# Loading the first pair of value heads as f32 over the two hardware DMA queues and casting it on GpSimd

## Chip, cores and metric

One NeuronCore of a Trainium2 chip. The metric is the device time of one execution in microseconds (us); lower is better.

## The reference, cut to what matters

```python
def _attn_ref(q, k, v, E, F):            # q, k, v: (8, 8, 1024, 64) f32; E, F: (64, 1024) f32
    k_proj = np.einsum('ks,bhsd->bhkd', E, k)
    v_proj = np.einsum('ks,bhsd->bhkd', F, v)
    scores = scale * np.matmul(q, k_proj.transpose(0, 1, 3, 2))
    ...                                   # softmax
    return np.matmul(attn, v_proj)

def _moe_ref(x, w_in, w_out):            # x: the 8192 x 512 result of the attention
    h = x @ w_in                          # w_in 512 x 2048
    g = h * np.clip(h + 3.0, 0.0, 6.0) / 6.0
    return g @ w_out                      # w_out 2048 x 512
```

A cheap attention with projected keys and values feeds two large matrix products. The products (lines 450 and 470 of the kernel before) fill TensorE from about 20 us to the end. The change touches only the loads of the first batch, by which the kernel gets to that point.

## The kernel before: the parts that matter

```python
    ef_f32 = consts.tile([P, S], f32, name="ef_f32")
    nc.sync.dma_start(out=ef_f32[:KP], in_=E)          # hardware queue of SyncE
    nc.scalar.dma_start(out=ef_f32[KP:], in_=F)        # hardware queue of ScalarE
    ...
    def load_pair(n, j):                               # GpSimd's queue: the DMA casts f32 to bf16
        hs = slice(2 * j, 2 * j + 2)
        nc.gpsimd.dma_start(out=kqv[0][n][:, hs], in_=kqv_dram[n][0][:, hs])

    for j in range(KO):                                # KO = 4 pairs of heads
        load_pair("k", j)
        load_q0(0, slice(2 * j, 2 * j + 2))
        ...
    for j in range(KO):
        load_pair("v", j)
    ...
    for lo, n in ((0, 128), (128, 128), (256, 256), (512, 256), (768, 256),
                  (1024, 512), (1536, 512)):
        load_w_in(lo, n)                               # also GpSimd's queue
    ...
            for j in range(KO):                        # First.first_block, cut
                self.keys(j)                           # needs k of pair j
                if j > 1:
                    sums(j - 2)
                self.queries(0, (j,))                  # needs q of pair j
                if j > 0:
                    scores(j - 1)
                ...
            self.vals(0, nc.vector.tensor_copy)        # needs v of pair 0
            ...                                        # vals(1), vals(2), products between them
            self.vals(3, nc.scalar.copy)
    # then the first matmul of x @ w_in (line 450), which needs the first piece of w_in
```

All loads that cast go by GpSimd's queue in this kernel; so all of q, k, v and the weights stand in one line, in the order of this code. "v0" below is v of the first pair of heads, "k3" is k of the last pair, and so on. The *start* is the time at which line 450 begins (457 in the changed kernel, whose lines are 7 lower). Some matmul records are missing from a trace: of the first two matmuls of this line, the profile before has only the second (20.68 us; the weights for both are loaded at 20.45). To compare like with like, "start" is the second one.

The softmax here doesn't subtract the row's maximum and nothing guards it: scores larger than these inputs give would overflow.

## Time and profile before

| | kernel before |
|---|---|
| time, median of the first 3 runs | 511.65 us (511.52 to 511.9) |
| span of the profiled run | 510.0 us, in a run of 511.81 us |
| TensorE busy | 497.4 us, 98% |
| start (first recorded matmul of line 450, its second) | 20.68 us |
| first piece of w_in landed | 20.41 us |

In the views PE is TensorE and PEld its weight loads, DVE is VectorE, ACT ScalarE, POOL GpSimd and SP SyncE; L450 is line 450 of the kernel. The lines of the page, of the chain, of the waits and of the first microseconds are in the prediction below. The point to take from them: after 20 us TensorE hardly ever waits, so the time of this kernel is, to a fraction of a microsecond, the start plus a constant. In the profiled run 511.81 - 20.68 = 491.13 us.

### The profile page before, as it was taken

Reading aid. Unit: us, or ns where it says so; the run is one execution under the profiler, and the core shown is the slowest. Engines: PE = TensorE matmul, PEld = TensorE weight load, DVE = VectorE, ACT = ScalarE, POOL = GpSimd, SP = SyncE. Lnnn points to the kernel's source line nnn. Section 1 sums busy time; section 2 is a strip of 40 time slices with the busy share of each in tenths; the row PEclk is TensorE's granted clock in tenths of the full one; section 3 lists DMA queues with packets and bytes.
Section 4 is the critical chain, followed back from the end, with each engine's and each line's share of the span. In section 5 each row is a group of like instructions: output and inputs, shape, how many; then the busy total and the mean of one; then the engine's idle time right before and its main releaser. Section 6 shows DMA issues by size and latency. Waiting matters only on the chain.

```text
span 510.0 us, 7106 instructions
## 1 busy us (share of the span) xinstructions
PE 497.4 (98%) x2750; PEld 224.3 (44%) x2802; DVE 257.5 (50%) x401; ACT 274.5 (54%) x493; POOL 37.9 (7%) x57
## 2 busy tenths in 40 slices
PE   8899999999899999999999999999999999999996
PEld 3444444444344444444444444444444444444442
DVE  3572735855655733656434743467444563334420
ACT  3657476567576545664466644674447654444431
POOL 8610020010100200002000020000000000000000
PEclk9999999999999999999999999999999999999999
DMA  9999999599299493516924188421110111101112
GB/s 165 199 205 207 202 156 236 97 159 176 88 184 186 91 218 76 125 41 91 225 57 94 52 141 169 107 58 33 42 41 25 38 42 42 42 21 42 41 51 74
DMA packets 74210, 55.39 MB, mean 109 GB/s; under 512 B 35520, under 2 KB 65984, under 8 KB 74176
## 3 DMA queue, kind: packets, MB, share of 16 engines
q0 software_dynamic: 31952, 29.36, 37.0%
q1 hardware_dynamic: 42000, 25.17, 19.4%
q10 hardware_dynamic: 224, 0.39, 0.3%
q8 instruction: 22, 0.36, 0.3%
q14 instruction: 12, 0.10, 0.1%
HBM read 59.24 MB, written 16.78 MB: 149 GB/s over the span
## 4 chain that ended last, share of the span: by engine, by line
PE 94%; DMA 3%; issue 1%; POOL 1%; DVE 0%; ACT 0%; DVEq 0%; POOLq 0%
PE mm L470 43%; PE mm L450 43%; PE at L181 3%; DMA w_in_sb<-in_moe_w_in_dram 2%; PE at L227 1%; PE mm L227 1%; DMA k<-in_k_dram 1%; PE at L209 1%; PE mm L209 0%; PE at L370 0%; POOL q L97 0%; DVE kp L187 0%; POOL k L101 0%; PE at L350 0%; DVE xT L246 0%
## 5 line engine op out<-in xcount | busy, mean ns | idle before, releaser
L456 DVE SCALAR_TENSOR_TENSOR g<-r,mm 128x512 bf16<-128x512 f32 x256 | 173.8, 686 | 131.8 <-ACT r L455 130.4
L470 PE MATMUL mm<-w_out_sb,g 128*128 128x512 bf16 x995 | 231.8, 379 | 1.7 <-issue 0.5
L450 PE MATMUL mm<-xT,w_in_sb 128*128 128x512 bf16 x1001 | 229.2, 379 | 3.1 <-DVE xT L246 1.2
L455 ACT ACTIVATE r<-mm 128x512 f32<-128x512 f32 x256 | 152.8, 599 | 76.2 <-PE mm L450 73.7
L450 PEld LDWEIGHTS <-w_in_sb 128*128 128x128 bf16 x1024 | 99.4, 98 | 124.0 <-issue 5.5
L470 PEld LDWEIGHTS <-g 128*128 128x128 bf16 x1024 | 98.0, 98 | 121.5 <-issue 7.2
L484 ACT COPY o_sb<-mm 128x512 f32<-128x512 f32 x35 | 20.3, 587 | 91.5 <-PE mm L470 91.5
L484 DVE COPY o_sb<-mm 128x512 f32<-128x512 f32 x28 | 19.3, 691 | 67.3 <-PE mm L470 64.2
L159 ACT ACTIVATE rec<-mm 128x512 f32<-128x512 f32 x34 | 19.0, 595 | 34.1 <-PE mm L227 17.6
L163 ACT ACTIVATE rec<-rec 128x512 f32<-128x512 f32 x60 | 35.6, 637 | 0.0
L246 DVE TENSOR_TENSOR xT<-at,rec 128x512 bf16<-128x512 f32 x44 | 28.1, 680 | 7.1 <-ACT rec L163 7.1
L218 ACT ACTIVATE aT<-at 128x512 bf16<-128x512 f32 x44 | 23.1, 613 | 0.9 <-PE at L209 0.9
L159 ACT ACTIVATE rec<-at 128x512 f32<-128x512 f32 x30 | 17.3, 598 | 6.0 <-PE at L227 3.7
L199 POOL COPY mark<-kT 1x1 bf16<-1x1 bf16 x5 | 0.9, 178 | 210.1 <-DMA kT<-kp 210.1
L181 PE MATMUL at<-k,e_t 128*64 128x512 bf16 x56 | 13.4, 382 | 0.0
L181 PE MATMUL at<-v,f_t 128*64 128x512 bf16 x56 | 13.4, 382 | 0.0
L187 DVE CAST kp<-at 64x512 bf16<-64x512 f32 x14 | 9.0, 678 | 4.9 <-PE at L181 4.9
L218 ACT ACTIVATE aT<-mm 128x512 bf16<-128x512 f32 x12 | 6.5, 594 | 8.9 <-PE mm L209 8.9
L190 DVE CAST vp<-at 64x512 bf16<-64x512 f32 x14 | 9.7, 694 | 0.4
L181 PEld LDWEIGHTS <-e_t 128*64 128x64 bf16 x56 | 5.6, 109 | 7.2 <-PE at L227 2.1
L479 DVE COPY o_sb<-mm 128x256 f32<-128x256 f32 x1 | 0.4, 425 | 16.0 <-PE mm L470 16.0
L227 PE MATMUL at<-aT,vp 64*64 64x512 bf16 x88 | 8.5, 376 | 0.0
(62 smaller groups left out, 147.0 us busy)
## 6 DMA issues: line engine op xcount, KB each, us to landing
out_dram<-o_sb SPq DMA_DIRECT2D x63, 256.0 KB, 2.0
k<-in_k_dram POOLq DMA_DIRECT2D x7, 1024.0 KB, 15.4
v<-in_v_dram POOLq DMA_DIRECT2D x7, 1024.0 KB, 21.0
q<-in_q_dram POOLq DMA_DIRECT2D x7, 1024.0 KB, 10.5
w_out_sb<-in_moe_w_out_dram POOLq DMA_DIRECT2D x4, 512.0 KB, 17.1
k<-in_k_dram POOLq DMA_DIRECT2D x4, 256.0 KB, 5.8
v<-in_v_dram POOLq DMA_DIRECT2D x4, 256.0 KB, 7.9
w_in_sb<-in_moe_w_in_dram POOLq DMA_DIRECT2D x2, 512.0 KB, 11.9
```

What stands on the lines that cost most here:

```text
L159: nc.scalar.activation(ln, den, AF.Ln)
L163: nc.scalar.activation(ln, ln, AF.Exp, scale=-1.0)
L181: nc.tensor.matmul(ps[e * KP:(e + 1) * KP], ef_t[e][:, so, :], kqv[self.b]["kv"[e]][:, :, so, :], start=(so == 0), stop=(so == SO - 1))
L190: nc.vector.tensor_copy(self.vp[a * KP:(a + 1) * KP], self.ps[KP:].rearrange("p (h d) -> p h d", d=D))
L218: nc.scalar.activation(self.aT[j][:, r].rearrange("p a n -> p (a n)"), tiles[r], AF.Exp, scale=scale)
L227: nc.tensor.matmul(tiles[t][c:c + D].rearrange("p (r n) -> p r n", r=2), stationary(r, 2 * j + a), self.aT[j][r:r + KP, :, a, :], start=Tr ...
L246: nc.vector.tensor_mul(self.xT[:, j, t, :], av[t], recs[t])
L450: nc.tensor.matmul(h_ps, w_in_sb[:, ko, fo * P:(fo + 1) * P], xT[:, ko, t, :], start=(ko == 0), stop=(ko == KO - 1))
L455: nc.scalar.activation(r, h_ps, AF.Relu, bias=0.5, scale=1.0 / 6.0)
L456: nc.vector.scalar_tensor_tensor(g[:, fo, :], r, 1.0, h_ps, op0=ALU.min, op1=ALU.mult)
L470: nc.tensor.matmul(o_ps, g[:, fo, c * P:(c + 1) * P], w_out_sb[:, fo, :], start=(fo == 0), stop=(fo == FO - 1))
L484: (copy or nc.scalar.copy)(o_sb, o_ps)
```

## The change

The intent: the hardware queues are idle after E and F, and the two GpSimd casts are cheap, so one pair of v can leave the crowded line of GpSimd's queue and everything behind it, w_in above all, can come earlier.

```diff
@@ -72,6 +72,11 @@
     nc.sync.dma_start(out=ef_f32[:KP], in_=E)
     nc.scalar.dma_start(out=ef_f32[KP:], in_=F)
+
+    v_f32 = []
+    for a, queue in enumerate((nc.sync, nc.scalar)):
+        v_f32.append(rpool.tile([P, TOK], f32, tag="r", name="r").rearrange("p (s d) -> p s d", s=SO))
+        queue.dma_start(out=v_f32[a], in_=kqv_dram["v"][0][:, a])
@@ -105,8 +110,10 @@
-    for j in range(KO):
+    for j in range(1, KO):
         load_pair("v", j)
+    for a in range(2):
+        nc.gpsimd.tensor_copy(kqv[0]["v"][:, a], v_f32[a])
```

## The prediction

> **What bounds the kernel now.** I read the page from the top: engine shares, slices, chain.
>
> ```profile
> PE 497.4 (98%) x2750; PEld 224.3 (44%) x2802; DVE 257.5 (50%) x401; ACT 274.5 (54%) x493; POOL 37.9 (7%) x57
> ...
> PE   8899999999899999999999999999999999999996
> ...
> DMA  9999999599299493516924188421110111101112
> ...
> PE 94%; DMA 3%; issue 1%; POOL 1%; DVE 0%; ACT 0%; DVEq 0%; POOLq 0%
> ```
>
> TensorE is busy for 98% of 510 us and holds 94% of the chain that ends last. Its only thin slices are the first two (12.75 us each) and the last. So a change to the very first loads can only move the moment at which TensorE begins its unbroken run, and everything after shifts by as much. The next view is therefore the chain of the first 24 us; columns are start, length, what.
>
> ```profile
> 4.73 6.02 DMA k<-in_k_dram
> 10.75 0.29 issue
> 11.04 9.37 DMA w_in_sb<-in_moe_w_in_dram
> 20.41 0.27 issue
> 20.68 0.38 PE mm L450
> ```
>
> The unbroken run starts at 20.68 us, released by the landing of the first piece of w_in at 20.41. That piece is issued at 11.04, when the third pair of k has landed (the program lets eight transfers of GpSimd's queue be open), but takes 9.37 us to land. It is not large (128 KB written as bf16): it stands in line behind what was issued before. The waits of TensorE between 14 and 24 us say how much that is worth.
>
> ```profile
> PE mm L450 <- DMA w_in_sb<-in_moe_w_in_dram: 0.7, 1, 0.7
> PE mm L370 <- ACT aT L390: 0.6, 1, 0.6
> PE mm L363 <- DVE kT L333: 0.3, 1, 0.3
> ```
>
> TensorE itself was ready 0.73 us before that landing: its timeline has the last matmuls of the values (line 338) at 19.33 for 0.62, so until 19.95. The front of the kernel thus has two chains that end almost together: the queue of loads (20.41) and the attention of the first block on TensorE, ScalarE and VectorE (19.95 plus a start).
>
> The stretches of the first microseconds (columns: window, its length, busy time and count of five engines, clock, DMA share, GB/s) show whether the transfer engines have room.
>
> ```profile
> 2.00:2.50 0.50, 0.50 (x3) 0.16 (x2) 0.00 (x0) 0.50 (x1) 0.50 (x2) 1.00 1.86 123
> 2.50:3.00 0.50, 0.50 (x2) 0.15 (x1) 0.00 (x0) 0.14 (x1) 0.49 (x2) 1.00 0.22 57
> 3.00:3.50 0.50, 0.50 (x2) 0.15 (x1) 0.00 (x0) 0.00 (x0) 0.43 (x2) 1.00 0.75 279
> 4.00:4.50 0.50, 0.50 (x3) 0.22 (x2) 0.00 (x0) 0.00 (x0) 0.50 (x2) 1.00 0.87 191
> 7.00:8.00 1.00, 0.93 (x10) 0.43 (x8) 0.42 (x1) 0.01 (x1) 1.00 (x2) 1.00 1.24 201
> ```
>
> From 4.5 us on the share is above 1 (packets overlap) and the rate is flat near 200 GB/s of bf16 written, which is 400 GB/s of f32 read. The engines are full; before 4.5 us there are holes.
>
> **What the Trainium skill says.** "DMA: Bandwidth & Descriptors", section "Issuing engines are not separate DMA queues": transfers begun by sync, scalar and gpsimd run on the same 16 engines and interleave, and several issuers only save issue time. Section "Queues, rings and completion order" of the same page: each engine takes packets in turn from the rows that have work. The trace agrees as far as it goes: the sum of the rates is flat while E, F and k are in flight together. "GPSIMD Engine Reference", section "4.1 Engine selection": one-input elementwise work is roughly line-rate on GpSimd, and section 3.1 gives 1.03 to 1.8 cycles an element at 1.2 GHz; the trace before has no such cast on GpSimd, only a memset of 128x128 in 0.23 us.
>
> **The change part by part.**
>
> 1. Removed: one of the four v loads of GpSimd's queue (0.74 us of issue at 7.58) and its place in the line. The landings (start plus time to landing, from the DMA issues of single windows) are k0 6.8, q0 7.6, k1 8.8, q1 9.5, k2 10.75, q2 11.5, k3 12.7, q3 13.4, v0 14.7, v1 16.0, v3 18.6, w_in 20.4 us. So one v pair takes 1.28 us of the line: 512 KB read in 1.28 us is 410 GB/s, the full rate.
>
> 2. Added: two loads of 256 KB f32 on the hardware queues, behind E and F. Issue costs 0.58 us on SyncE and on ScalarE, both idle then (both wait for E and F until 6.11). E's packets of 4 KB take 159 ns once the stream runs (my reading of the raw packet records), which is 412 GB/s over 16 engines: the same time for each byte read as the casting loads. So the same 1.28 us of engine time is still needed, only earlier: it is not taken away from the front of the kernel, because it is drawn from the same full engines before w_in. Only what falls into the holes is free. The holes from 2.5 to 4.5 us are 0.5 x (0.78 + 0.25 + 0 + 0.13) = 0.58 us; E needed 0.8 us from the end of its issue to its first packet, so the new load, issued until 1.9 us, cannot fill the first of them: I choose 0.25 us filled, with 0 to 0.5 possible. First piece of w_in: 20.41 - 0.25 = about 20.15 us.
>
> 3. Moved: k and q of all pairs come after (or between) the packets of v0, so they are late by 1.28 - 0.25, about 1.0 us: k0 7.8, q0 8.6, k1 9.8, q1 10.5, k2 11.75, k3 13.7, q3 14.4. Against the starts on TensorE: keys of pair 0 at 8.01 (k0 in time), of pair 1 at 9.70 (0.1 to 0.3 late), of pair 2 at 11.39 (0.4 to 0.6), of pair 3 at 13.01 (0.7 to 0.9). But after the keys of pair 3 TensorE waited 0.61 us for ScalarE until 14.26, and that wait absorbs the delay: keys 13.8 to 14.4, the sums at once after it, queries at 14.8 instead of 14.59. Left over: 0.2 to 0.45 us, call it 0.3. The chain on TensorE then ends at 19.95 + 0.3 = 20.25. The v pairs 1 to 3 keep their times less the filled hole (14.7 is passed by v0, which is already there), so they do not add.
>
> 4. Two casts of 128x512 f32 to bf16 on GpSimd. With the skill's 1.03 to 1.8 cycles, an estimate: 512 x 1.03 to 1.8 / 1.2 GHz = 0.44 to 0.77 us, plus a start, say 0.75 each. The compiled order puts them after the v issues and before w_in. The last v issue now waits for k1 (9.8) and ends at 10.5; casts until 12.0; then w_in is issued at 12.0, not 11.04. Cost on the path: none, since the line in front of it lasts until about 18.5; there are some 6 us of room. The values' first use is at 15.94, 4 us later. One slot fewer in the eight open transfers also means that w_in now waits for q1, not k2; that is earlier than the casts and does not count.
>
> 5. The r buffers: both loads sit in two of four buffers of r, free since 12 us, first wanted at 22.66. No cost.
>
> Sum: TensorE starts its run at the later of w_in (20.15 + 0.27) and its own chain (20.25 + some 0.2), so near 20.45 instead of 20.68: 0.2 us earlier, 0.04% of 511.65. Later loads keep their order and total. The first w_out chunk lands at 20.69 + 14.5 = 35.2 and is wanted at 35.66, so that small gain is not lost there. Predicted: 511.5 us.
>
> **The rivals.**
>
> A. The gain is real: v0 leaves the line, holes and slack hide its bytes, and w_in lands 1.28 us earlier. For it: the 0.73 us wait is measured. Against: the share above 1 from 4.5 us on. Even then TensorE was ready only at 19.95, so at most 0.7 us: 510.9.
>
> B. A wait takes the place: v0's packets push F and the first k and q back by the full 1.3 us (two hardware rows against one software row, no hole used). F landed at 6.05, 1.1 us after E, and starts the whole chain (casts at 6.11). If F is late by 0.5 to 1 us and k3 by 1.3, TensorE's chain ends at 20.8 to 21.2 and w_in no longer matters: plus 0.3 to 0.7, 511.9 to 512.4.
>
> C. GpSimd becomes the bound: a cast of over 3 us would delay w_in beyond its place in the line and the whole weight stream with it. Nothing in the trace speaks for it, a memset of a quarter of the columns took 0.23 us; if so, plus 1 to 3 us.
>
> D. Nothing moves at all: filled holes go to nobody because the slower chain is TensorE's. 511.6 to 511.7.
>
> **Range and chances.** The three mechanisms span 510.9 to 512.4; three runs before spread over 0.4 us, and another chip may differ by that again. I take 510.7 to 512.6. A 2% effect would be 10.2 us, half of the whole front of the kernel; only a hang-like wait on GpSimd's queue could do it. Faster 0.005, same 0.985, slower 0.01.
>
> **What would show it.** Right: the landing of the first w_in within 0.5 us of 20.4 in spite of v0's absence from its queue; k3 and q3 landing about 1 us later than 12.7 and 13.4; casts under 1 us, ended by about 12.5; the first matmul of line 450 (then a few lines lower) between 20.2 and 20.9; TensorE's wait for w_in shrunk or gone. Wrong: keys and queries landing as before (then A: the engines had room), E or F landing late by over 0.5 us (B), w_in issued after 16 us (C), or a new gap in TensorE's run after 21 us, which none of my steps contains.

## The result, and the profile after

The changed kernel is correct. Its median is 511.94 us (511.64 to 512.38, six runs) against 511.5 us for the kernel before in the same rounds; the ratio is 1.0008, 95% interval 0.9995 to 1.0021. (Ratios here are the mean time of one kernel's fast runs over that of the other's of the same rounds, so not quite the ratio of the medians quoted.) By the 2% rule it is "same". The slower state with a lower clock, which some executions of a program show, did not occur.

The interval holds 1, so this alone settles no sign. Over the whole study the kernel before ran 33 times (511.16 to 511.9, median 511.46) and the changed one 13 times (511.64 to 512.38, median 511.92). In each of the three sets of rounds that have both, the changed kernel's median is above, by 0.44, 0.45 and 0.75 us. I take about 0.45 us as the likely cost of the change; the profiles say where it would come from.

The page of the changed kernel, the lines that answer to those in the prediction:

```profile
PE 497.5 (98%) x2750; PEld 224.5 (44%) x2802; DVE 257.9 (51%) x401; ACT 274.4 (54%) x493; POOL 38.3 (8%) x58
...
PE   7999999999899999999999999999999999999996
...
DMA  9999989599199493515914188421110111101112
...
PE 95%; DMA 1%; issue 1%; POOL 1%; DVE 1%; ACT 0%; DVEq 0%; POOLq 0%
```

One digit of TensorE moved, the first (8 to 7 tenths of 12.75 us); and in the chain "DMA" fell from 3% to 1%. The chain of the first 24 us shows why (start, length, what; the pieces left out are matmuls and copies of the first attention block):

```profile
4.72 7.28 DMA k<-in_k_dram
12.00 0.04 issue
12.05 0.63 PE at L329 x8
12.68 0.35 PE mm L377 x2
13.03 0.02 issue
13.05 0.61 ACT rec L166
13.66 0.02 issue
13.68 0.63 ACT o_sb L403
14.31 0.56 ACT aT L397 x2
14.87 0.04 issue
14.91 0.40 PE mm L377 x2
...
20.04 0.55 PE at L345 x8
20.60 0.12 issue
20.71 0.38 PE mm L457
```

Before, the chain went from k to the *issue of w_in* and along the load line. Now it goes from the landing of k2 (12.00 us; 10.75 before) into the keys of pair 2 on TensorE, and from there through the whole attention block to the values of pair 3 and the start. The load line has not got shorter: w_in's first piece was issued at 12.13 us and took 8.3 us, so it landed at 20.43, as before (20.41), with v0 gone from in front of it.

TensorE's waits, first 24 us of the changed kernel (total us, times, longest):

```profile
PE at L329 <- DMA k<-in_k_dram: 1.1, 4, 0.6
...
PE mm L377 <- ACT aT L397: 0.3, 1, 0.3
PE mm L370 <- DVE kT L340: 0.3, 1, 0.3
```

The wait for w_in (0.7 us) is gone, and a wait for all four k pairs (1.1 us in sum) is there that the kernel before does not have. And the transfer engines in the same stretches as in the prediction, with one more (window, length, busy of five engines, clock, DMA share, GB/s):

```profile
2.00:2.50 0.50, 0.50 (x3) 0.16 (x2) 0.00 (x0) 0.25 (x1) 0.50 (x2) 1.00 1.66 172
2.50:3.00 0.50, 0.50 (x2) 0.15 (x1) 0.00 (x0) 0.50 (x1) 0.49 (x2) 1.00 0.14 41
3.00:3.50 0.50, 0.50 (x2) 0.15 (x1) 0.00 (x0) 0.50 (x1) 0.44 (x2) 1.00 0.93 336
4.00:4.50 0.50, 0.50 (x3) 0.22 (x2) 0.00 (x0) 0.00 (x0) 0.50 (x2) 1.00 1.13 254
4.50:5.00 0.50, 0.50 (x3) 0.22 (x2) 0.00 (x0) 0.00 (x0) 0.50 (x2) 1.00 0.88 184
...
7.00:8.00 1.00, 0.68 (x7) 0.29 (x5) 0.42 (x1) 0.25 (x1) 0.60 (x1) 1.00 1.28 225
```

The loads of v0 filled the holes at 3.0 and 4.0 us (share 0.75 to 0.93, 0.87 to 1.13), but a new one opened at 4.5 us (1.18 before, 0.88 now), and the one at 2.5 us stayed. In sum nothing shows as gained: the landing of w_in is the same.

GpSimd's timeline (start, length, instruction) shows the casts:

```profile
8.48 1.43 POOL L106 DMA_DIRECT2D v<-in_v_dram  x2 [0.88 <-DMA k<-in_k_dram]
...
11.00 1.18 POOL L116 CAST v<-r 128x512 bf16<-128x512 f32 x2
...
12.13 3.74 POOL L127 DMA_DIRECT2D w_in_sb<-in_moe_w_in_dram  x5
```

Two casts take 1.18 us, and the whole detour ends 4.4 us before the values of pair 0 are wanted (16.59 us).

Where the delay builds up, before and after, from the two timelines and the landings (start plus time to landing), in us:

| | before | changed | later by |
|---|---|---|---|
| F landed | 6.05 | 5.74 | -0.3 |
| k0 landed; keys of pair 0 start | 6.8; 8.01 | 8.2; 8.24 | 1.4; 0.2 |
| k1; keys of pair 1 | 8.8; 9.70 | 10.0; 10.14 | 1.2; 0.4 |
| k2; keys of pair 2 | 10.75; 11.39 | 12.0; 12.05 | 1.25; 0.7 |
| k3; keys of pair 3 | 12.7; 13.01 | 13.95; 13.96 | 1.25; 0.95 |
| sums of pair 1 (after ScalarE's exponentials) | 14.26 | 14.91 | 0.65 |
| values of pair 0, of pair 3 start | 15.94; 19.33 | 16.59; 19.98 | 0.65; 0.65 |
| first piece of w_in landed | 20.41 | 20.43 | 0.0 |
| start | 20.68 | 20.71 | 0.0 |

In this pair of profiles the delay of TensorE's own chain, 0.65 us, just used up the 0.73 us for which TensorE had waited for w_in. That would make a difference of zero, and the spans are indeed equal (510.0 and 510.0). But the profile before fell in a run of 511.81 us, slow for that kernel. The experiments start there.

### The profile page after: what moved, and what is told of

Read it like the earlier page. It is cut to its first block, busy times and chain, and to the rows that moved or that the text cites. A ratio compares the mean times of both kernels' runs of the same rounds, so it can differ in the third digit from the quotient of the medians.

```text
span 510.0 us, 7113 instructions
## 1 busy us (share of the span) xinstructions
PE 497.5 (98%) x2750; PEld 224.5 (44%) x2802; DVE 257.9 (51%) x401; ACT 274.4 (54%) x493; POOL 38.3 (8%) x58
## 3 DMA queue, kind: packets, MB, share of 16 engines
q1 hardware_dynamic: 42144, 25.43, 19.1%
## 4 chain that ended last, share of the span: by engine, by line
PE 95%; DMA 1%; issue 1%; POOL 1%; DVE 1%; ACT 0%; DVEq 0%; POOLq 0%
PE mm L477 43%; PE mm L457 43%; PE at L188 3%; PE at L234 1%; PE mm L234 1%; DMA k<-in_k_dram 1%; PE at L216 1%; PE at L377 0%; PE at L345 0%; PE mm L216 0%; POOL q L102 0%; DVE kp L194 0%; PE at L357 0%; PE mm L377 0%; POOL k L106 0%
## 5 line engine op out<-in xcount | busy, mean ns | idle before, releaser
L491 ACT COPY o_sb<-mm 128x512 f32<-128x512 f32 x35 | 20.3, 587 | 91.5 <-PE mm L477 91.5
L491 DVE COPY o_sb<-mm 128x512 f32<-128x512 f32 x28 | 19.3, 691 | 67.3 <-PE mm L477 64.3
## 6 DMA issues: line engine op xcount, KB each, us to landing
v<-in_v_dram POOLq DMA_DIRECT2D x7, 1024.0 KB, 20.7
w_out_sb<-in_moe_w_out_dram POOLq DMA_DIRECT2D x4, 512.0 KB, 17.0
w_in_sb<-in_moe_w_in_dram POOLq DMA_DIRECT2D x2, 512.0 KB, 11.9
```

The costliest lines, as they stand in the source:

```text
L491: (copy or nc.scalar.copy)(o_sb, o_ps)
```

## The experiments

Theory 1: the start waits for the later of two chains, the load line (ending with w_in) and TensorE's own attention block (starting with the keys); the bytes of v0 cost the same 1.28 us of the full transfer engines wherever they stand; the change moves them ahead of the keys, so it delays the second chain and leaves the first alone. Rivals: the load line bounds both kernels; the hardware loads are hidden in idle time; GpSimd's casts hold things up.

### The changed kernel again

No edit.

> The changed kernel again, with more rounds. Theory (two chains end together; the change moved the bound from the load line to TensorE's own chain): start of the first line-of-w_in matmul 20.7 us within 0.1, ratio to the kernel before 1.0000 within 0.001. Rival (the change costs some 0.4 us, as the first six runs hint): ratio 1.0007 or more with an interval that leaves out 1.

511.91 us (511.9 to 512.03, five runs) against 511.46 (511.16 to 511.85, nine): ratio 1.0007, 0.9994 to 1.0021. Start at 20.86 us (both first matmuls are recorded here, the first at 20.64), waits for k 1.0 us. The theory's expectation of no difference failed; the rival's, of an interval without 1, was not met either, though no run of one kernel overlaps those of the other in this set. In this profile the first piece of w_in landed at 12.34 + 7.0 = 19.3 us, a microsecond earlier than in the first profile of the same kernel, and the start was still 20.86. So here the load line did not bind at all; TensorE's own chain did.

### The kernel before, three more profiles, and the changed kernel beside them

No edits.

> The kernel before once more, unedited, for a second profile of it. So far its one profile is of a run of 511.81 us, near the slow end of its times (511.16 to 511.9), and in it the first piece of w_in lands at 20.4 us because one transfer engine spent 0.95 us on a 16 KB fetch of instructions from 18.26 us on. Theory: in a run near its median (511.3 to 511.5) that piece lands by 19.9 us and the start is TensorE's own chain, at 20.2 to 20.4 us, with no wait for w_in; the changed kernel's start of 20.6 to 20.7 then accounts for its 0.45 us. Rival: the start is 20.7 in all runs of it, and the 0.45 us arises elsewhere.

> As the look before it: start of line 450 and time move together, time less 491.1 us is the start (511.81 less 20.68), within 0.15 us, so a run of 511.4 starts at 20.3.

> As the two looks before it; three profiles of the kernel before should show at least one start below 20.45 us if the theory holds, and none if the rival does.

> The changed kernel once more on the same chip as the three looks. Theory: TensorE waits some 1.0 us for keys, the values of pair 3 start at 20.0 to 20.2, the run starts at 20.6 to 20.75 wherever the fetch falls, time 511.8 to 512.0.

| profile | time of that run | 16 KB fetch begins | v3 landed | w_in, first piece | values of pair 2 start | start |
|---|---|---|---|---|---|---|
| before, first | 511.81 | 18.2 | 18.5 | 20.4 | 17.78 | 20.68 |
| before, look 1 | 511.38 | 17.8 | 18.4 | 20.0 | 17.65 | 20.25 |
| before, look 2 | 511.45 | 17.5 | 19.6 | 19.8 | 17.55 | 20.32 |
| before, look 3 | 511.38 | 17.4 | 19.5 | 19.7 | 17.25 | 20.21 |
| changed, first | 511.77 | 18.4 | 18.5 | 20.4 | 18.43 | 20.71 |
| changed, again | 511.9 | 18.8 | 18.7 | 19.3 | 18.64 | 20.86 |
| changed, look | 512.1 | 18.7 | 18.5 | 20.8 | 18.52 | 21.06 |

What was expected of the start and the time of the kernel before held: all three looks start at 20.2 to 20.3 us, and time less start is 491.13 to 491.17 us in them. The reason given did not hold: look 1 expected TensorE's own chain to set the start, without a wait for a load, but in all four profiles of the kernel before a load comes last (w_in in the first and in look 1, v3 in looks 2 and 3).

The expectation for the changed kernel failed in part. The wait for keys (0.9 us) and the values of pair 3 (20.06 us) were as expected, but the start of 21.06 and the times of 512.1 and 512.24 us are later than the 20.6 to 20.75 and 511.8 to 512.0 expected "wherever the fetch falls". In this profile w_in's first piece landed at 20.8 us. The view of the waits puts TensorE's wait down to VectorE; the timeline of the weight loads (PEld), which come first, shows that it was for w_in:

```profile
PE mm L457 <- DVE xT L406: 0.4, 1, 0.4
```

```profile
20.83 0.11 PEld L457 LDWEIGHTS <-w_in_sb 128*128 128x128 bf16 x2 [0.33 <-DMA w_in_sb<-in_moe_w_in_dram]
```

(Look 1 is alike: VectorE by the first view, 0.37 us for w_in by the second.) So with the change the two chains nearly tie, and a late w_in can still hold up the start.

The mean start is 20.37 before and 20.88 after, 0.51 us apart; the times of these seven runs are 0.42 us apart on average, so the start accounts for the cost. The column "values of pair 2" is TensorE's own chain, before any late load can touch it: mean 17.56 before, 18.53 after, so **the change delays that chain by 1.0 us**; about half of it shows in the start, because the kernel before spends the other half waiting for loads. That wait is, as said, not always the wait for w_in. In look 3 TensorE waited for v3 instead (first the waits from 0 to 60 us, then the chain of 15 to 24 us):

```profile
PE at L338 <- DMA v<-in_v_dram: 0.7, 1, 0.7
```

```profile
9.70 9.79 DMA v<-in_v_dram
19.49 0.05 issue
19.54 0.62 PE at L338 x8
20.16 0.05 issue
20.21 0.38 PE mm L450
```

The cause of the wandering lateness seems to be a fetch of instructions that shares the transfer engines: one packet of 16 KB in the queue named "instruction". Here are the queues of the kernel before from 17.5 to 20 us (packets, MB, share of 16 engines):

```profile
q0 software_dynamic: 1353, 0.45, 160.3%
q8 instruction: 1, 0.02, 2.4%
```

2.4% of 16 engines for 2.5 us is 0.95 us of one engine. Where it began at 17.4 or 17.5 us, v3 landed about 1.1 us later than in the other two profiles; where it began at 17.8 or 18.2, v3 did not, and w_in landed later (20.0 and 20.4 us instead of 19.7 and 19.8). In the changed kernel w_in landed a microsecond earlier where the fetch began last (18.8 us). The Trainium skill, "Runtime: NRT & Kernel Launch", section "Instruction fetch mechanics", has instructions fetched ahead in blocks of 16 KiB by a DMA queue of the sequencer and calls the cost mostly hidden. The size agrees; the cost is not hidden here, where a full line of loads runs at the edge of the path. This is a coincidence in time in seven profiles, not an intervention: I could not move the fetch by itself.

### No v0 at all

```diff
-        queue.dma_start(out=v_f32[a], in_=kqv_dram["v"][0][:, a])      # and the tiles
+    nc.vector.memset(kqv[0]["v"][:, :2], 0.0)
-        nc.gpsimd.tensor_copy(kqv[0]["v"][:, a], v_f32[a])
```

> Wrong result on purpose: the changed kernel with both new loads and both casts taken out, the first pair of v zeroed early by VectorE. It shows what the bytes of v0 cost. Theory: v0 takes 1.28 us of the full transfer engines wherever it stands, so keys and queries land as in the kernel before (k3 12.7 us), the first piece of w_in about 19.1 us, and TensorE's run starts when its own chain ends, at 20.1 to 20.3 us: 0.4 to 0.6 us faster than either kernel, ratio near 0.999. Rival (the loads are hidden in idle time of the engines): no change, start at 20.7, w_in at 20.4.

Its output is wrong, which doesn't matter for the time. 510.89 us, ratio 0.9986 (0.9974 to 0.9999): 0.57 us faster than the kernel before, and 1.0 us faster than the changed one. The profile (of its fastest run, 510.58) starts at 19.45 us (first matmul 19.23), without a wait for k. The size in time is as expected, the start earlier than the expected 20.1 to 20.3, because TensorE's own chain without the late loads is faster than I had read from the first profile (values of pair 2 at 17.23, as in look 3). w_in missed its expectation too: it landed at 17.8 us, not 19.1, which was 20.41 less 1.28. The 20.41 was a late landing: there w_in came 1.9 us after v3, here 0.7 us after the last v pair (17.1 us). The transfer of v0 is not hidden.

### The same bytes added to the kernel before

```diff
+        queue.dma_start(out=v_f32[a], in_=kqv_dram["v"][0][:, a])      # both, never read
```

> The kernel before with the two new loads added but not used (the pair still comes by GpSimd's queue too): 512 KB more. Theory (no holes are filled): everything behind lands 1.28 us later, the first piece of w_in at 21.7, keys as in the changed kernel (k3 near 14.0), start at 21.9 to 22.0: plus 1.2 us, ratio 1.002 to 1.0025. If holes took some of it, the landing of w_in falls short of 21.7 by that amount. Rival (hidden): start at 20.7.

512.7 us, ratio 1.0023 (1.001 to 1.0035): plus 1.24 us for 512 KB, which at the rate of the v pairs is 1.28 us. The first piece of w_in landed at 12.5 + 9.2 = 21.7 us, the start was 21.9, both as expected, and the waits for k were 1.1 us. So no part of these bytes shows as taken by holes. The changed kernel is this one with 1.28 us of line taken back behind the keys.

### Two pairs by the hardware queues

```diff
-    for a, queue in enumerate((nc.sync, nc.scalar)):
+    for a, queue in enumerate((nc.sync, nc.scalar, nc.sync, nc.scalar)):
-    for j in range(1, KO):   ...   for a in range(2):
+    for j in range(2, KO):   ...   for a in range(4):
```

> The change done for two pairs of v instead of one: four loads on the hardware queues, four casts on GpSimd. Theory: the first piece of w_in stays at 20.4, but keys and queries come another 1.0 to 1.3 us later (k3 about 15.2), and as the slack of TensorE's chain was used up by the first pair, the start moves one for one, to 21.6 to 22.0: plus 0.9 to 1.3 us, ratio about 1.002. Rival (load line still the bound): start stays at 20.7, ratio 1.000.

513.04 us (512.77 to 513.95), ratio 1.0034 (1.0021 to 1.0046): plus 1.6 us, more than the expected 0.9 to 1.3. Twice the bytes ahead of the keys cost about three times as much, as a chain whose slack is used up should. Its waits, first 24 us:

```profile
PE at L329 <- DMA k<-in_k_dram: 1.8, 2, 1.4
...
PE at L357 <- DMA q<-in_q_dram: 0.6, 1, 0.6
```

In this profile w_in's first piece had landed at 19.1 us (issued at 13.1, 6.0 to land), and the start was 22.85: the load line is out of it. The profile is of a run of 513.74 us in which TensorE's clock was at half from 11.2 to 14.6 us, after the long waits for k and q, which adds to it; the three of its five runs at full mean clock took 512.77 to 513.04, plus 1.3 to 1.6 us.

### w_in's first 256 columns in two halves, without and with the change

```diff
-    for lo, n in ((0, 128), (128, 128), (256, 256), ...
+    for ko in (0, 2):
+        nc.gpsimd.dma_start(out=w_in_sb[:, ko:ko + 2, :256], in_=w_in_v[:, ko:ko + 2, :256])
+    for lo, n in ((256, 256), ...
```

> The kernel before, with the first 256 columns of w_in loaded as two halves of the contraction (rows of 1 KB) instead of two pieces of 128 columns (rows of 512 B). Nothing else. Theory (there the load line is the last chain, by 0.73 us): the first half lands at 19.3 to 19.8 instead of 20.4, TensorE's wait for w_in goes, start at 20.1 to 20.3, 0.4 to 0.6 us faster, ratio near 0.999. Rival (the small pieces land late only because the line in front is long): start stays at 20.6 to 20.7.

> The same two halves of w_in in the changed kernel. Theory (there TensorE's own chain, delayed by late keys, is the last one, the load line only ties with it): w_in lands as early as in the run above but the start stays at 20.7 within 0.15 us, ratio 1.000. Rival (the load line is what bounds the changed kernel too): start at 20.2, the same gain as above.

| | pieces of 128 columns | two halves |
|---|---|---|
| kernel before | 511.48 (511.29 to 511.57) | 511.43, ratio 1.0000 (0.9987 to 1.0013) |
| with the change | 511.91 (other set of rounds) | 512.01, ratio 1.0012 (0.9999 to 1.0024), to the kernel before |

The first expectation failed: the time is that of the kernel before. In its profile the first half landed at 19.9 us, v3 was late (TensorE waited 0.6 us for it, as in looks 2 and 3) and the start is 20.42 (first matmul 20.20), near that of the kernel before in most profiles. My baseline of 20.68 was the exception. Of the second expectation the time held: no gain, start 20.96 (first matmul 20.73). But w_in landed at 20.7 us there, not as early as in the other run, and the first weight load waited 0.30 us for it, so this run does not separate the two chains. The change costs 0.6 us with the halves, about what it costs with the pieces (0.44 to 0.75).

### v0's loads held back behind the other v pairs

```diff
-        queue.dma_start(out=v_f32[a], in_=kqv_dram["v"][0][:, a])       # at the top
+        nc.gpsimd.memset(v_f32[a][:, :1, :1], 0.0)                      # after the v issues: the DMA waits for it
+        nc.sync.dma_start(out=v_f32[a], in_=kqv_dram["v"][0][:, a])
+        if i == 4:                                                      # casts before the fifth piece of w_in
+            for a in range(2):
+                nc.gpsimd.tensor_copy(kqv[0]["v"][:, a], v_f32[a])
```

> The changed kernel, but its two loads are held back until GpSimd has issued the other v pairs (near 10 us), both on SyncE's queue, the casts moved behind the fourth piece of w_in. Theory (the early packets of v0 are what makes the keys late): k0, q0, k1 and k2 land as in the kernel before (6.8, 7.6, 8.8, 10.75), TensorE's waits for k shrink from 1.1 us to under 0.3, w_in again at 20.4 and TensorE waits for it again, some 0.3 to 0.7 us; start 20.7. Time as both kernels, ratio 1.000. Rival (keys are late for another reason, such as one slot less in GpSimd's queue or the casts): waits for k stay near 1 us.

514.82 us, ratio 1.0065 (1.0051 to 1.0078): plus 3.3 us, far from the expected 1.000. The first half held: no wait for k is left, keys and queries are as early as before, so it is v0's early packets that make them late and not the slot in GpSimd's queue. The second half failed. Waits of TensorE and the granted clock (last columns: clock, DMA share, GB/s):

```profile
PE at L346 <- POOL v L131: 1.7, 1, 1.7
```

```profile
16.00:17.00 1.00, 0.00 (x0) 0.00 (x0) 0.00 (x0) 0.95 (x4) 0.12 (x2) 1.00 1.22 222
17.00:18.00 1.00, 0.38 (x5) 0.38 (x4) 0.00 (x0) 0.00 (x0) 1.00 (x2) 0.62 1.43 206
18.00:19.00 1.00, 1.00 (x8) 0.49 (x6) 0.29 (x1) 0.00 (x0) 1.00 (x3) 0.50 1.73 170
```

The loads, issued at 9.9 and 10.3 us, moved their first packet at 13.5 us and landed at 15.3 and 16.9. Issued while the engines were full, they began 3.6 us after the issue and then got about half of them (by the packet records of 14 to 15 us, 186 KB beside 198 KB read for GpSimd's queue). The casts came 1.7 us too late for the values, TensorE stood still for that time, and its clock was at half for 3.4 us, from 17.2. The experiment answers the question on the keys; its time says nothing on the change.

### Six more casts on GpSimd

```diff
+    again = consts.tile([P, TOK], bf16, name="again")
+    for i in range(6):
+        nc.gpsimd.tensor_copy(again.rearrange("p (s d) -> p s d", s=SO), v_f32[i % 2])
```

> The changed kernel with six more casts of the same shape (into a scratch tile) after the two: GpSimd then issues w_in near 15.7 instead of 12.1 us. Theory (the line in front of w_in lasts until about 18.5 us, so the cast's time is off the path): w_in still lands at 20.4, start 20.7, ratio 1.000. Rival (GpSimd's casts are what holds the changed kernel up): start moves by 3.5 us, ratio 1.007.

513.74 us (512.53 to 514.48), ratio 1.0044 (1.0032 to 1.0057): plus 2.3 us over the kernel before, neither expectation. The start did not move (20.68 us), so the first piece of w_in had the room that I gave it. But the later pieces had not: all seven are now issued from 16.1 to 21.3 us, and TensorE waits for them after the start (0.8 us until 23.7, 0.3 until 29.5; the rest of the 2.3 us was not traced to its causes). The rows compare the kernel before, then this one:

```profile
20.00:24.00 4.00, 3.32 (x16) 1.43 (x18) 1.60 (x4) 1.59 (x4) 2.36 (x4) 1.00 1.43 198
```

```profile
20.00:24.00 4.00, 3.18 (x22) 1.38 (x21) 2.28 (x5) 1.44 (x4) 3.81 (x6) 1.00 1.09 134
```

From 20 to 24 us the engines move 134 instead of 198 GB/s. Why the line stays slow with several pieces open is not settled. For the change itself it shows that the two real casts (1.18 us) are not on the path, and that the six microseconds of room in the prediction were true for the first piece only.

## Why the prediction was right or wrong

The time lies in the range and the class is right, but the sign of the small effect was not: 0.2 us faster predicted, about 0.45 us slower measured. That the time fell into the range says little for the mechanism: the range, 1.9 us wide, held both signs. The signs listed as "right" came true in the first pair of profiles (w_in at 20.43 us, keys over 1 us late, casts ended at 12.2, start at 20.71, no wait for w_in), but they do not tell a delay that is absorbed from one that is passed on. By its own steps:

- **Step 1, the price of v0's bytes (1.28 us at the full rate): right.** Adding the same bytes cost 1.24 us.
- **Step 2, holes that take 0.25 us of it: wrong, no part of it shows.** w_in landed at 20.43 with the change in the paired profiles, the last v pair at 18.5 to 18.7 us with it and at 18.4 or 18.5 without (where the fetch does not touch it), and the added bytes cost their full price. A hole in the DMA share at one moment was not room here: what was filled at 3 and 4 us opened again at 4.5.
- **Step 3, keys late by 1.0 us, 0.3 of it left on TensorE's chain: the step that failed.** The keys came 1.2 to 1.4 us late in the first pair of profiles and 1.4 to 1.7 in the means of all seven, more than 1.0 and more than v0's 1.28; why more is open. But the main error is the absorption: I counted TensorE's wait for ScalarE before the sums (0.61 us) as slack. ScalarE is fed by what follows the same keys: its exponentials of pair 1 stand behind its work on the sums of pair 0, and TensorE does these after the keys of pair 2 (the chain above, 12.00 to 14.91 us). They moved from 13.57 to 14.22 us, the wait only shrank to 0.34, and the sums of pair 1 came 0.65 us later. Over all profiles the chain is 1.0 us later, not 0.3.
- **Step 4, the casts off the path: right.** 1.18 us for both (616 ns each, slightly overlapped) against 1.5 estimated; one is inside the 0.44 to 0.77 us that the skill's cycles give; w_in issued at 12.13 against 12.0.
- **Step 5, the r buffers: right**, no wait on them appears.
- **The base of the sum.** The start of 20.68 and the slack of 0.73 us came from one profile, of a run 0.35 us slower than the median. (The prediction counts the 0.73 us to the landing of w_in; they run to the start, and from 19.95 to the landing at 20.41 it is 0.46.) The kernel before usually starts at 20.2 to 20.3. This made the predicted start of 20.45 look like a gain.
- **Rivals.** A (the gain) is out: the load line is as long as before. B came closest, with its plus 0.3 to 0.7 us, and for its reason as to k; its part on F is wrong, F landed at 5.7 to 5.9 us in the profiles of the changed kernel and at 5.5 to 6.1 before; E, F and the two loads landed one after another (4.5, 5.7, 6.2 and 8.0 us). C is out for two casts. D is out as well.

What stays open: whether the fetch of instructions is the cause of the wandering lateness, why the keys are later than v0's bytes alone would make them, and the slow line with eight casts. The 0.45 us itself rests on medians, on profiles and on the order of every set, not on an interval that leaves out 1.

No version with a correct result beats the kernel before: 511.43 against 511.48 us with w_in in halves is no difference.

## What to carry to other kernels

Here, with the transfer engines full most of the time from 4.5 us on, another queue added no room: it changed the order, and the loads put early on the idle queues went ahead of loads that were wanted sooner. Ask of such a change which loads it overtakes. Before counting a wait as slack, follow its releaser back: if it is fed by the thing that gets later, the wait moves along instead of absorbing. And for effects below a microsecond take several profiles of the kernel before, compare the time of the profiled run with the median of all, and check that the record that you compare is the same instruction in each.

## What the Trainium skill lacked or had wrong

- "Runtime: NRT & Kernel Launch" (section "Instruction fetch mechanics") calls crossing a 16 KiB block mostly hidden. Here one such packet held one of 16 engines for 0.95 us beside a full line of loads; a load of that moment landed some 1.1 us late, and starts of one kernel moved from 20.2 to 20.7 us. (A coincidence in seven profiles, not an intervention.)
- "DMA: Bandwidth & Descriptors" (section "Specifications") gives a first byte of about 0.6 us for hardware queues. It does not say how much later it is under full engines: a load issued at 9.9 us moved its first packet at 13.5 us.
- "TensorE: Matmul & The Clock Gate" (Part 1, "HAM oscillation") gives as the rule that TensorE should have no idle gaps above some 3.4 us. Here the clock was halved for 3.4 us without such a gap, twice: in the run with the loads held back from 17.2 us, 1.3 us into a standstill of 1.7, and in the run with two pairs from 11.2 us, where the longest of the waits before had been 1.4 us, until 8.7. In the 3.4 us before, TensorE was busy for 1.4 and 1.7 us. (The page also tells of one kernel in which frequent short idle times did it, without a number for how short.)
- "GPSIMD Engine Reference" has no measured one-input cast from f32 to bf16: 128x512 took 616 ns, two of them 1.18 us.
